# Attention and two expert layers in one kernel: the first batch's values loaded by ScalarE's queue, its keys by SyncE's

## The chip, the cores and the metric

The kernel runs on 1 core of one Trainium2 chip. The metric is the device time of one execution in microseconds (us). Three runs of the kernel before gave 496.34, 498.15 and 498.86 us, so the median is 498.15 us.

## The reference

Three parts follow each other. `q`, `k` and `v` have 4 batches, 8 heads, 576 positions and 64 values per head, all float32. Linear attention with a norm comes first, then a layer with a skip test and 8 experts (hidden size 1024), then a second layer with 8 experts and a capacity per expert. Only the first part is near the change:

```python
def _attn_ref(q, k, v, g_norm) -> np.ndarray:
    kv = np.einsum('bhsd,bhse->bhde', k, v)
    out = np.einsum('bhsd,bhde->bhse', q, kv)
    rms = np.sqrt(np.mean(out * out, axis=-1, keepdims=True) + 1e-06)
    return (out / rms * g_norm).astype(np.float32)
...
x = np.ascontiguousarray(attn_out.transpose(0, 2, 1, 3)).reshape(B * S, H * D)
x = _moe_ref(x=x, **moe_kwargs)
return _moe2_ref(x=x, **moe2_kwargs)
```

## The kernel before, in words

All keys of one batch are a table of 576 rows by 512 columns (8 heads side by side), and so are all values. A row of either is 2048 bytes. `load_kv(b)` brings one batch into SBUF: rows 0 to 511 of the keys go into the tile `wraw` (called `k0` in the code) as four chunks of 128 rows, the last 64 rows into the tile `k` (`k1`), and the values go the same way into another `wraw` (`v0`) and into `v` (`v1`). For the first batch each chunk is a DMA of its own of 256 KB, keys and values by turns; for the later batches a DMA holds two chunks. `load_q(b)` then brings the batch's queries, already transposed, as one DMA of 128 rows of 9216 bytes. All these DMAs are issued by SyncE (SP), in the order of the code: first batch, its queries, second batch, and so on. The order in which a queue issues is the order of the program; nothing here is placed by a planner.

ScalarE (ACT) issues two small DMAs at the start, `au` (gate weights and norm, 128 rows of 532 bytes, L116) and `cap_i` (the capacity, 8 bytes that are read once for each of 128 partitions, L118). Its first arithmetic of the attention is the copy at L701.

TensorE's order is written out by hand. It begins with ten matmuls on zeros (`warm`, L111), then does `emit_kv(0, range(5))` (L698): for chunks 0 to 3 and the last 64 rows, values against keys, summed in one PSUM tile. So each chunk needs its keys and its values. After the fifth chunk ACT copies the sums out (L701, L702), `emit_kvT` (L710, L713) transposes them and multiplies them with the gate weights, ACT copies these results (L715, L716), and `emit_products` (L732) multiplies queries with them, a tile of 128 rows at a time. The chunks of batch 1 are placed between the tiles of batch 0. VectorE (DVE), ACT and GpSimd (POOL) norm each tile, and SP stores it. The routing of the first expert layer starts while batch 3 is still in work, and the two expert layers fill the rest of the time.

Of the kernel before, what the change touches and what calls it, by code (L numbers as in the profile page):

```python
# [47 lines left out]
def moe_kernel(ctx: ExitStack, tc: tile.TileContext, qT, kk, vv, aux, w1a, w2a, w1b, w2b, capacity, out):  # L48
    nc = tc.nc
# [47 lines left out]
    for m, caps in ((1, CAP1), (2, CAP2)):  # L97
        t = cst.tile([1, E], F32, name=f"capc{m}")
# [538 lines left out]
    with att:  # L637
        warm(p1u.tile([128, 512], F32, name="acc"), 10)
        kvbd_all, vk_all = [], []
        for i in range(2):  # L640
            kvbd_all.append(asp0.tile([128, 4, 162], F32, name=f"kvbd{i}"))
            t = asp0.tile([128, 4, 128], F32, name=f"vk{i}")
# [5 lines left out]
        def load_kv(b):  # L648
            k0 = wr_p.tile([128, 2048], F32, name="wraw").rearrange("p (c d) -> p c d", c=4)
            v0 = wr_p.tile([128, 2048], F32, name="wraw").rearrange("p (c d) -> p c d", c=4)  # L650
            k1 = akv.tile([64, D], F32, name="k1")
            v1 = akv.tile([64, D], F32, name="v1")
            step = 1 if b == 0 else 2
            for c in range(0, 4, step):
                for t, src in ((k0, kk), (v0, vv)):
                    nc.sync.dma_start(out=t[:, c:c + step, :], in_=src[b, 0:512].rearrange("(c p) d -> p c d", c=4)[:, c:c + step, :])
            nc.sync.dma_start(out=k1, in_=kk[b, 512:576])
            nc.sync.dma_start(out=v1, in_=vv[b, 512:576])
            kt[b], vt[b] = (k0, k1), (v0, v1)

        def load_q(b):
# [7 lines left out]
        for b in range(B):  # L669
            load_kv(b)  # L670
            load_q(b)
# [97 lines left out]
        with tc.manual_schedule(engines={mybir.EngineType.PE}):  # L769
# [38 lines left out]
            for b in range(B):  # L808
                t = list(range((b * S) // 128 if b else 0, ((b + 1) * S) // 128))
                for u in ATT_SEQ[b].split():  # L810
# [13 lines left out]
                    elif u == "E":  # L824
                        p = tc.cur_priority
# [44 lines left out]
    with first_mix:  # L870
# [11 lines left out]
        for i in range(2):  # L882
            t = cst.tile([128, NB1, E], BF16, name=f"o2_{i}")
# [277 lines left out]
        step = tc.manual_schedule(engines={mybir.EngineType.PE})  # L1161
# [265 lines left out]
```

## Time and profile before

| | |
|---|---|
| runs before, us | 496.34, 498.15, 498.86 (median 498.15) |
| profiled execution, its own time | 496.94 us |
| its span, first to last instruction | 495.3 us |
| TensorE busy in the span | 472.5 us (95%) |
| mean granted TensorE clock | 0.982 of full |
| VectorE, ScalarE, GpSimd busy | 303.4, 205.8, 146.0 us |
| moved by DMA | 104.90 MB, 212 GB/s on average |

The table holds averages over the whole program. The change touches its first microseconds only, so the views to read are those of single stretches: who is busy, at what clock, what the DMA queues moved, and what the chain of work waited for. Queue q1 in the rows is the one that SP issues on, q10 the one that ACT issues on.

### The profile page before, as it was taken

Reading aid. Unit: us, or ns where it says so; the run is one execution under the profiler, and the core shown is the slowest. Engines: PE = TensorE matmul, PEld = TensorE weight load, DVE = VectorE, ACT = ScalarE, POOL = GpSimd, SP = SyncE. Lnnn points to the kernel's source line nnn. Section 1 sums busy time; section 2 is a strip of 40 time slices with the busy share of each in tenths; the row PEclk is TensorE's granted clock in tenths of the full one; section 3 lists DMA queues with packets and bytes.
Section 4 is the critical chain, followed back from the end, with each engine's and each line's share of the span. In section 5 each row is a group of like instructions: output and inputs, shape, how many; then the busy total and the mean of one; then the engine's idle time right before and its main releaser. Section 6 shows DMA issues by size and latency. Waiting matters only on the chain.

```text
span 495.3 us, 10239 instructions
## 1 busy us (share of the span) xinstructions
PE 472.5 (95%) x3824; PEld 450.7 (91%) x3829; DVE 303.4 (61%) x945; ACT 205.8 (42%) x524; POOL 146.0 (29%) x179
## 2 busy tenths in 40 slices
PE   6998778999999999999999999999999999999995
PEld 3897667999999999999998899999999999999984
DVE  2157978658767675265776576565657566675711
ACT  1376551344433532114233364454545545555400
POOL 5288584203021131113025230240604124040201
PEclk8599999999999999999999999999999999999999
DMA  8999495999768676358218993564656556400001
GB/s 236 362 356 347 163 355 154 315 323 348 269 229 299 206 290 210 126 194 314 91 45 304 414 336 142 193 202 150 214 187 221 201 179 215 144 37 2 35 23 41
DMA packets 24617, 104.90 MB, mean 212 GB/s; under 512 B 3609, under 2 KB 4761, under 8 KB 15984
## 3 DMA queue, kind: packets, MB, share of 16 engines
q1 hardware_dynamic: 17264, 77.75, 45.6%
q0 software_dynamic: 7008, 26.35, 15.1%
q8 instruction: 32, 0.52, 0.4%
q14 instruction: 25, 0.20, 0.1%
q10 hardware_dynamic: 288, 0.07, 0.1%
HBM read 92.15 MB, written 12.76 MB: 212 GB/s over the span
## 4 chain that ended last, share of the span: by engine, by line
PE 83%; DVE 8%; DMA 3%; ACT 2%; issue 2%; POOL 1%; SPq 0%; POOLq 0%; DVEq 0%; ACTq 0%
PE hp L592 14%; PE yp L1089 8%; PE yp L1091 8%; PE yp L1090 7%; PE hp L1089 6%; PE hp L1090 6%; PE hp L1091 6%; PE yp L626 6%; PE yp L616 6%; PE yp L617 2%; PE tp L1276 2%; PE yt L1320 2%; PE ops L732 2%; PE tp L1011 1%; PE tp L574 1%
## 5 line engine op out<-in xcount | busy, mean ns | idle before, releaser
L979 ACT CAST whi<-wraw 128x512 fp32r<-128x512 f32 x152 | 86.1, 619 | 73.3 <-PE yp L1090 30.1
L980 DVE TENSOR_TENSOR wlo<-wraw,whi 128x512 fp32r<-128x512 f32 x152 | 97.4, 684 | 26.1 <-ACT whi L979 25.0
L339 POOL DMA_INDIRECT rows<-xcat,gi x40 | 41.7, 1042 | 135.8 <-ACT ex L348 85.3
L1089 PE MATMUL hp<-xh,whi 128*128 128x256 f32 (+7 forms) x256 | 78.8, 308 | 0.2 <-DVE hl L1109 0.2
L592 PE MATMUL hp<-xT,wraw 128*128 128x128 f32 (+8 forms) x576 | 78.1, 292 | 0.5 <-ACT xT L576 0.5
L1091 PE MATMUL hp<-xh,wlo 128*128 128x256 f32 (+7 forms) x256 | 76.7, 299 | 0.0
L1090 PE MATMUL hp<-xl,whi 128*128 128x256 f32 (+7 forms) x256 | 76.6, 299 | 0.0
L592 PEld LDWEIGHTS hp<-xT,wraw 128*128 128x128 f32 x576 | 73.4, 190 | 2.9 <-issue 1.8
L1310 POOL DMA_INDIRECT out<-ot,toki x24 | 35.2, 1466 | 83.5 <-DVE su L352 39.5
L1089 PE MATMUL yp<-hh,whi 128*128 128x320 f32 (+5 forms) x192 | 58.8, 306 | 0.0
L1090 PE MATMUL yp<-hl,whi 128*128 128x320 f32 (+5 forms) x192 | 57.3, 298 | 0.0
L1091 PE MATMUL yp<-hh,wlo 128*128 128x320 f32 (+5 forms) x192 | 57.2, 298 | 0.0
L1089 PEld LDWEIGHTS hp<-xh,whi 128*128 128x128 f32 x256 | 48.3, 189 | 0.8 <-DVE hl L1109 0.5
L1090 PEld LDWEIGHTS hp<-xl,whi 128*128 128x128 f32 x256 | 48.3, 189 | 0.0
L1091 PEld LDWEIGHTS hp<-xh,wlo 128*128 128x128 f32 x256 | 48.3, 189 | 0.0
L1027 POOL DMA_INDIRECT xcat<-rows,toki x16 | 16.4, 1026 | 95.5 <-DVE mxt L297 93.1
L616 PE MATMUL yp<-hT,whi 128*128 128x352 f32 (+4 forms) x160 | 43.1, 351 | 0.0
L1108 ACT ACTIVATE hh<-hp 128x320 fp32r<-128x320 f32 (+8 forms) x64 | 27.2, 429 | 31.7 <-PE hp L1091 24.1
L1109 DVE SCALAR_TENSOR_TENSOR hl<-hp,hh 128x320 fp32r<-128x320 f32 (+8 forms) x64 | 30.0, 475 | 13.4 <-ACT hh L1108 12.8
L617 PE MATMUL yp<-hT,wlo 128*128 128x176 f32 (+4 forms) x160 | 37.7, 235 | 0.0
L1090 PEld LDWEIGHTS yp<-hl,whi 128*128 128x128 f32 x192 | 36.2, 189 | 0.0
L1089 PEld LDWEIGHTS yp<-hh,whi 128*128 128x128 f32 x192 | 36.2, 188 | 0.0
(255 smaller groups left out, 867.2 us busy)
## 6 DMA issues: line engine op xcount, KB each, us to landing
wraw<-in_w1a SPq DMA_DIRECT2D x14, 1024.0 KB
wraw<-in_w2a SPq DMA_DIRECT2D x14, 1024.0 KB, 5.6
wraw<-in_w1b SPq DMA_DIRECT2D x14, 1024.0 KB
wraw<-in_w2b SPq DMA_DIRECT2D x14, 1024.0 KB, 5.2
xcat<-xr SPq DMA_DIRECT2D x18, 264.0 KB, 3.9
q<-in_q SPq DMA_DIRECT2D x3, 1152.0 KB
wraw<-in_k SPq DMA_DIRECT2D x6, 512.0 KB, 10.2
wraw<-in_v SPq DMA_DIRECT2D x6, 512.0 KB, 12.8
```

Of the source, the lines that this page charges most:

```text
L339: return nc.gpsimd.indirect_dma_start(out=rows[:n], out_offset=None, in_=xcat[0:source], in_offset=bass.IndirectOffsetOnAxis(ap=gi[:n], ax ...
L592: nc.tensor.matmul(hp[:, ff, :], lhsT=wv[:, fc % 4, k, :], rhs=XT[j][:, k, c0:c1], start=(k == 0), stop=(k == 3))
L616: nc.tensor.matmul(yp, lhsT=wh[:, fc, :], rhs=HT[j][:, fc], start=(fc == 0), stop=False, skip_group_check=True)
L617: nc.tensor.matmul(yp[:, 0, :], lhsT=wl[:, fc, :], rhs=HT[j][:, fc, 0, :], start=False, stop=(fc == 7), skip_group_check=True)
L626: nc.tensor.matmul(yp[:, dd, :], lhsT=wv[:, dd, fc, :], rhs=HT[j][:, fc, c0:c1], start=(fc == 0), stop=(fc == 7))
L979: nc.scalar.copy(out=hi[:, cs], in_=raw[:, cs])
L980: ins = nc.vector.tensor_tensor(out=lo[:, cs], in0=raw[:, cs], in1=hi[:, cs].bitcast(F32), op=ALU.subtract)
L1089: nc.tensor.matmul(ps, lhsT=wh, rhs=xh, start=first, stop=False)
L1090: nc.tensor.matmul(ps, lhsT=wh, rhs=xl, start=False, stop=False)
L1091: nc.tensor.matmul(ps, lhsT=wl, rhs=xh, start=False, stop=last)
L1109: ev = nc.vector.scalar_tensor_tensor(out=hl[:, fs, cs], in0=hp, scalar=0.0, in1=hh[:, fs, cs].bitcast(F32), op0=ALU.max, op1=ALU.subtract)
L1310: st = nc.gpsimd.indirect_dma_start(out=out, out_offset=bass.IndirectOffsetOnAxis(ap=r2["toki"][:nn, j, bi:bi + 1], axis=0), in_=ot[:nn], ...
```

## The change

In `load_kv`, for the first batch alone, the four chunks of the values and their last 64 rows are issued by ACT instead of SP. The keys of the first batch, the queries and all later batches stay with SP. An empty line is added, so line numbers below it are one higher in the changed kernel.

```diff
             step = 1 if b == 0 else 2
             for c in range(0, 4, step):
                 for t, src in ((k0, kk), (v0, vv)):
-                    nc.sync.dma_start(out=t[:, c:c + step, :], in_=src[b, 0:512].rearrange("(c p) d -> p c d", c=4)[:, c:c + step, :])
+
+                    (nc.scalar if b == 0 and t is v0 else nc.sync).dma_start(out=t[:, c:c + step, :], in_=src[b, 0:512].rearrange("(c p) d -> p c d", c=4)[:, c:c + step, :])
             nc.sync.dma_start(out=k1, in_=kk[b, 512:576])
-            nc.sync.dma_start(out=v1, in_=vv[b, 512:576])
+            (nc.scalar if b == 0 else nc.sync).dma_start(out=v1, in_=vv[b, 512:576])
```

SP's first instructions in the kernel before, at the start of the program (`k_209`, `v_210` are the last 64 rows of batch 0, `q_221` its queries, 128x2x512 a double chunk of batch 1):

```order
L656 DMA wraw<-in_k 128x512
L656 DMA wraw<-in_v 128x512
...
L657 DMA k_209<-in_k 64x512
L658 DMA v_210<-in_v 64x512
L664 DMA q_221<-in_q 128x2304
L656 DMA wraw<-in_k 128x2x512
```

The same place on SP in the changed kernel:

```order
L657 DMA wraw<-in_k 128x512 x4
L658 DMA k_209<-in_k 64x512
L665 DMA q_221<-in_q 128x2304
L657 DMA wraw<-in_k 128x2x512
L657 DMA wraw<-in_v 128x2x512
```

The five DMAs of the values are gone from SP, and the queries are its 6th DMA instead of its 11th.

ACT's first instructions in the changed kernel (the two copies of `vk_197` are its first arithmetic of the attention):

```order
L116 DMA au<-in_aux 128x133
L114 ACT_TABLE_LOAD
L114 ACTIVATE act_127<-eps_123 128x1
L118 DMA cap_i<-in_capacity 128x2
L657 DMA wraw<-in_v 128x512 x4
L659 DMA v_210<-in_v 64x512
L702 COPY vk_197<-acc 64x4x64
L703 COPY vk_197<-acc 64x4x64
```

The five DMAs stand behind `au` and `cap_i` and ahead of the first copy; the order of all other instructions, on every engine, is as before.

## Rows read from the trace of the kernel before

**Rows 1.** The page: span, and granted TensorE clock in 40 slices.
```profile
span 495.3 us, 10239 instructions
...
PEclk8599999999999999999999999999999999999999
```

**Rows 2.** Chain that ended last, 0 to 32 us: start us, us, what.
```profile
1.79 5.35 DMA wraw<-in_k
...
7.16 5.16 DMA v<-in_v
...
17.52 2.53 PE ops L732 x8
...
26.75 1.30 PE ops L732 x8
```

**Rows 3.** Timeline, 0 to 14 us: start us, us, engine, line; in brackets idle before, releaser.
```profile
0.87 0.41 ACTq L116 DMA_DIRECT2D au<-in_aux  x1
...
1.37 0.40 ACTq L118 DMA_DIRECT2D cap_i<-in_capacity  x1
...
3.21 0.43 SPq L656 DMA_DIRECT2D wraw<-in_v  x1
...
6.07 0.77 PE L698 MATMUL acc<-wraw 128*64 128x64 f32 x16
...
7.16 0.48 SPq L658 DMA_DIRECT2D v<-in_v  x1
...
7.68 0.58 SPq L664 DMA_DIRECT2D q<-in_q  x1
...
11.09 1.12 PE L698 MATMUL acc<-wraw 128*64 128x64 f32 x16 [0.94 <-DMA wraw<-in_v]
...
12.46 1.12 PE L698 MATMUL acc<-k,v 64*64 64x64 f32 x16 [0.25 <-DMA v<-in_v]
...
13.68 0.37 ACT L701 COPY vk<-acc 64x256 f32<-64x256 f32 x1 [10.87 <-PE acc L698]
```

**Rows 4.** DMA queues, 0 to 6 us: packets, MB, share of 16 engines.
```profile
q1 hardware_dynamic: 340, 0.63, 47.7%
q10 hardware_dynamic: 288, 0.07, 6.9%
```

**Rows 5.** DMA queues, 4 to 6 us.
```profile
q1 hardware_dynamic: 102, 0.18, 64.3%
q10 hardware_dynamic: 105, 0.00, 2.5%
```

**Rows 6.** DMA queues, 2.3 to 3.4 us.
```profile
q1 hardware_dynamic: 131, 0.24, 62.8%
q10 hardware_dynamic: 134, 0.06, 29.9%
```

**Rows 7.** DMA packets, 6 to 10 us.
```profile
DMA packets 880, 1.59 MB, mean 398 GB/s; under 512 B 102, under 2 KB 102, under 8 KB 880
```

**Rows 8.** DMA packets, 10 to 11.5 us.
```profile
DMA packets 117, 0.37 MB, mean 245 GB/s; under 512 B 25, under 2 KB 25, under 8 KB 92
```

**Rows 9.** DMA queues, 12 to 13.5 us.
```profile
q1 hardware_dynamic: 66, 0.61, 97.3%
```

**Rows 10.** Stretches: us, PE, PEld, DVE, ACT, POOL busy (x), PEclk, DMA share, GB/s.
```profile
5.92:13.58 7.66, 4.53 (x81) 3.91 (x82) 2.38 (x15) 0.00 (x0) 5.26 (x22) 0.75 1.05 356
13.58:17.52 3.94, 3.25 (x13) 2.59 (x14) 0.00 (x0) 1.59 (x4) 0.00 (x0) 0.50 1.01 384
17.52:23.35 5.83, 5.83 (x45) 5.38 (x46) 1.57 (x4) 1.58 (x4) 2.03 (x2) 0.50 1.07 344
31.00:43.00 12.00, 11.95 (x171) 11.14 (x170) 6.90 (x18) 8.86 (x25) 10.52 (x10) 1.00 1.02 331
43.00:61.00 18.00, 12.89 (x129) 11.18 (x131) 17.54 (x63) 9.65 (x28) 11.19 (x11) 1.00 0.67 235
...
78.00:495.00 417.00, 408.88 (x3201) 396.73 (x3200) 256.34 (x786) 169.61 (x430) 96.50 (x87) 1.00 0.56 195
```

## The prediction, made before the changed kernel ran

> **What bounds the kernel now.** I read the page first, then the chain that ended last, the timeline of the first 14 us, the DMA queues in short windows, and the table of stretches.
>
> The page says that the program is one long stretch of TensorE work at full clock, with a dip of the granted clock in its second slice [rows 1]. The table of stretches shows where a delay at the start could be lost: from 78 us to the end TensorE is busy 408.88 of 417 us, from 31 to 43 us 11.95 of 12, and between them, from 43 to 61 us, VectorE 17.54 of 18 [rows 10]. There is little idle time on whichever engine sets the pace, so I expect a microsecond lost before 30 us to arrive at the end nearly whole.
>
> The chain of the first 17 us is made of loads: it runs through a key chunk, issued at 1.79 us, and then through the last 64 rows of the values, issued at 7.16 us and waited for until 12.32 us [rows 2]. The first chunk's matmuls start at 6.07 us, the fourth chunk's wait 0.94 us for the values, and the fifth's 0.25 us more [rows 3]. What follows (sums copied out, transposes, first products at 17.52 us) is a chain in which nothing waits for a DMA.
>
> Two things about the DMAs matter. From 6 to 10 us they are full: 1.59 MB at 398 GB/s [rows 7]. Before 6 us they are not: SP's queue has moved 0.63 MB and ACT's 0.07 MB [rows 4]. In the last 2 us of that, the two queues moved 102 and 105 packets, with only 0.18 MB in all [rows 5]; the packets of ACT's queue are here the 8-byte reads of `cap_i`. In 2.3 to 3.4 us, with 2048-byte packets on SP's queue and 532-byte ones on ACT's, it was 131 and 134 [rows 6]. So while both queues have work, they advance packet for packet, whatever the packets' sizes. That is what the forecast rests on.
>
> **The change part by part.** (1) Five issues leave SP. With them gone the queries are SP's 6th DMA. The 6th was issued at 3.21 us without a stall, while the 10th and 11th (last values, queries) came at 7.16 and 7.68 us [rows 3]. So the queries are in SP's queue by about 3.7 us, before the DMAs are full. As issue time SP's saving is worth nothing: from 6 us on the DMAs have no idle time that earlier issues could fill [rows 7].
>
> (2) Five issues are added to ACT, each about 0.43 us as on SP, 2.2 us together, from 1.77 us (the end of the `cap_i` issue) to about 4 us. ACT's first copy waits 10.87 us for TensorE and starts at 13.68 us [rows 3], so they are hidden. Without that cover they would cost at most the 2.2 us.
>
> (3) The order in which the bytes arrive changes, and this is the term. Keys and values of the batch are 576 rows of 2048 bytes each, 1.18 MB each; the queries are 1.18 MB in 128 packets of 9216 bytes, 8 for each of the 16 DMA engines. Before, one queue delivered everything in the order of need. By 6.00 us 0.63 MB of 2.36 MB was there [rows 4]; the other 1.73 MB take 4.35 us at 398 GB/s [rows 7], to 10.35 us. The window with the 64-row transfers and the first query packets ran at 245 GB/s instead of 398 [rows 8], which loses 1.5 x (398 - 245) / 398 = 0.58 us, so to 10.9 us. The wait ended at 12.32 us [rows 2]: the slowest engine was 1.4 us behind that mean.
>
> After, the values stand behind `au` and `cap_i` in ACT's queue, and these 288 packets are through only at 6 us [rows 4]. SP's queue will have moved the same 0.63 MB by then, but all of it keys. From 6.00 us:
> - The other 0.55 MB of keys go packet for packet with 0.55 MB of values: 1.10 MB, 2.76 us, to 8.76 us. Then 0.63 MB of values are left, 308 packets.
> - SP's next work is the queries. Their 128 packets go with 128 value packets: 1.18 + 0.26 = 1.44 MB, 3.62 us, to 12.4 us. That a query packet does cost what its size says is seen where they run alone: 66 packets took 97.3% of 16 engines for 1.5 us, 0.35 us each [rows 9].
> - The 180 value packets left go with 180 of batch 1's keys: 0.74 MB, 1.85 us, to 14.2 us; with the same 0.58 us for the 64-row transfers, 14.8 us.
>
> If no engine is behind that mean, the last values are 14.8 - 12.32 = 2.5 us later; if the slowest is again 1.4 us behind, 3.9 us. The engines fell behind before 6 us, when the values have not begun, and the exchange packet for packet lets an engine that is behind with its keys go on with its values. I take 2.6 us, near the lower end. From below, nothing excludes a gain: if the values kept their place and the tail went away, they would be there 1.4 us sooner (10.9 instead of 12.32). The ends of this term are so -1.4 and +3.9 us.
>
> (4) From there the work is the same, 2.6 us later: the fifth chunk at about 15.1 us and the first products at about 20.1 us instead of 17.52. The granted clock is at 0.50 (1.2 GHz) in the stretches 13.58 to 17.52 us and 17.52 to 23.35 us, and TensorE had idle time in the first and none in the second before the clock rose [rows 10]. The same products take 2.53 us at that level and 1.30 us at the full one [rows 2]. If the clock rises later by as much as the uninterrupted work starts later, the whole 2.6 us are carried on. If it rises at 23.35 us as now, 2.6 us of work at the half level are replaced by work at the full one, and 1.3 us remain.
>
> (5) The loads of the later batches keep their order, and SP reaches them earlier. They bring the same bytes; batch 1's keys come beside the end of the values, and their matmuls are moved back too. I cost this at nothing.
>
> The sum is +2.6 us. The profiled execution took 496.94 us, with a span of 495.3 us, which is 1.2 us below the median of 498.15 us. It would become 499.5 us; for a median of runs I add the same to 498.15 us and forecast 500.8 us.
>
> **The rivals.**
> - **Half of it:** the delay is there, but the clock rises at the old moment, so 1.3 us remain: 499.5 us. For it: the profile shows two levels with a late rise, not a rise tied to an instruction. Against it: the rise came only after a stretch without any idle time, and the small wait for ACT before the products would then lie later.
> - **No change:** the place of the values in the transfers isn't moved, since the engines have the same bytes to bring; 498.15 us. Against it: the equal packet counts. The Trainium skill, "DMA: Bandwidth & Descriptors", section "Issuing engines are not separate DMA queues", has this rule: DMAs started by different engines run on the same 16 engines and interleave, and starting them from several saves only the issue time. By that rule nothing would be gained, and that the full window has no room for issue time agrees [rows 7]; the rule doesn't say what the interleaving does to the one transfer that is waited for.
> - **Faster:** SP's last value issue at 7.16 us was late because SP's queue was held up, and with two queues the last values are out by 4 us. If the exchange leaves them ahead of the queries, they land at 10.9 us and 1.4 us are gained: 496.75 us. If TensorE then also has fewer pauses between 5.92 and 13.58 us (it is busy 4.53 of 7.66 us there) and its clock stays up, the 9.08 us of busy time in the two stretches at 0.50 shrink by up to 4.5 us: 492.2 us [rows 10]. The point from which it decides is whether the values are through before the queries. For it: each chunk's keys and values travel side by side. Against it: in SP's queue only 36 packets of keys per engine stand ahead of the queries, so packet for packet they are reached before the values' 36 are done.
> - **Slower still:** the tail of 1.4 us stays too, 3.9 us are lost and carried whole: 502.05 us.
>
> **How the numbers follow.** The forecast has 0.38, half of it 0.20, no change 0.17, faster 0.14, slower still 0.11. A measurement of this kernel can tell about 0.5%, 2.5 us, from no change, so the border lies at 500.6 us. The forecast is a hair above it: I give 0.28 of its 0.38 to the slower side, with the 0.11 of the last rival 0.39. Half, no change and the small form of the faster case (0.05) make, with the forecast's other 0.10, 0.52. The large form of the faster case is 0.09. The range reaches from 497.4 us (the faster case's small gain in part, and the scatter of the runs) to 502.6 us (the last rival, and some scatter); it leaves out the large gain and the far end above.
>
> **What would show it.** Right: queue q10 in the changed profile holds some 1.2 MB, moved mostly between 6 and 15 us; in that time q1 moves the queries; the fourth and fifth chunks' matmuls wait for values by over 2 us more, the first chunk starts after 7 us, and the first products come at about 20 us. The chain then runs through a value DMA issued by ACT. Wrong: the last values landing before 12.3 us, or equal landing with the time changed. A delay at 20 us that is gone at 78 us would show step (4) wrong, and a wait of the first copy on ACT for anything but TensorE would show step (2) wrong.

## The result, and the profile after

The changed kernel took 501.11 us (median of 5 runs, 500.58 to 501.79). The kernel before took 497.51 us (5 runs, 496.34 to 498.86). The ratio is 1.007, with a 95% interval of 1.0043 to 1.0098: slower by 3.6 us. A second measurement, `e11_changed_again` below, gave 1.009 (1.0064 to 1.0116).

The page of the changed kernel, first the span, then the two queues (packets, MB, share of 16 engines):

```profile
span 498.9 us, 10244 instructions
...
q1 hardware_dynamic: 16608, 76.57, 44.7%
...
q10 hardware_dynamic: 944, 1.25, 0.7%
```

The span is 3.6 us longer than in [rows 1], and ACT's queue q10 now carries 1.25 MB: the change does what it says. The first 23 us of the changed kernel's timeline answer to [rows 3] (start us, us, engine; "q" behind an engine marks its DMA issues):

```profile
0.88 1.82 SPq L657 DMA_DIRECT2D wraw<-in_k  x4
...
1.81 0.45 ACTq L657 DMA_DIRECT2D wraw<-in_v  x1
...
3.94 0.33 SPq L665 DMA_DIRECT2D q<-in_q  x1
...
4.12 0.33 ACTq L657 DMA_DIRECT2D wraw<-in_v  x1
...
6.12 0.33 ACTq L657 DMA_DIRECT2D wraw<-in_v  x1
...
8.30 0.33 ACTq L657 DMA_DIRECT2D wraw<-in_v  x1
...
8.67 0.53 ACTq L659 DMA_DIRECT2D v<-in_v  x1
...
8.78 1.13 PE L699 MATMUL acc<-wraw 128*64 128x64 f32 x16 [2.85 <-DMA wraw<-in_v]
...
13.28 1.12 PE L699 MATMUL acc<-wraw 128*64 128x64 f32 x16 [3.38 <-DMA wraw<-in_v]
...
16.27 1.12 PE L699 MATMUL acc<-wraw 128*64 128x64 f32 x16 [0.59 <-DMA wraw<-in_v]
...
17.32 1.12 PE L699 MATMUL acc<-k,v 64*64 64x64 f32 x16
...
18.55 0.37 ACT L702 COPY vk<-acc 64x256 f32<-64x256 f32 x1 [15.72 <-PE acc L699]
...
22.39 2.53 PE L733 MATMUL ops<-kvbd,q 128*128 128x162 f32 x8 [0.36 <-ACT kvbd L717]
```

Two things are to be seen. TensorE waits for values at four of the five chunks; the fifth chunk begins at 17.32 instead of 12.46 us, the first products at 22.39 instead of 17.52 us, 4.87 us later. And ACT does not issue its value DMAs one behind the other: after the first at 1.81 us they come at 4.12, 6.12, 8.30 and 8.67 us, while the queries leave SP at 3.94 us.

The trace also has what spaces the issues. The loads of this program signal their landing on eight semaphores (counters that a landing DMA raises and an instruction can wait for), which SP and ACT share and use in turn. In every run, the first eight loads of the two engines together go out without a wait, and in the 14 us looked at each further one goes only when the load that had its semaphore before has landed. In the kernel before, the eight were six of SP and two of ACT; in the changed kernel they are five of SP and three of ACT. SP's waits, in the kernel before (0 to 8 us):

```profile
SPq L656 <- DMA au<-in_aux: 0.4, 1, 0.4
```

and in the changed kernel (0 to 14 us):

```profile
SPq L657 <- DMA wraw<-in_v: 2.6, 1, 2.6
...
SPq L665 <- DMA wraw<-in_k: 0.6, 1, 0.6
```

The first and the second are issues of SP that wait for a load of ACT; the third is the queries, which wait for the first key chunk. ACT's issues at 4.12, 6.12 and 8.30 us follow in the same way the landings of the gate weights and of SP's second and third key chunk, which were issued at 0.88, 1.33 and 1.80 us and took 3.2, 4.8 and 6.5 us to land.

The DMA queues of the changed kernel show what that does. From 0 to 6 us (against [rows 4]):

```profile
q1 hardware_dynamic: 337, 0.62, 46.6%
q10 hardware_dynamic: 294, 0.08, 6.5%
```

From 7.6 to 8.5 us:

```profile
q1 hardware_dynamic: 124, 0.34, 128.5%
q10 hardware_dynamic: 11, 0.01, 3.3%
```

From 9 to 11 us:

```profile
q1 hardware_dynamic: 73, 0.66, 82.7%
q10 hardware_dynamic: 71, 0.15, 19.3%
```

Until 6 us SP's queue moved 0.62 MB, all keys, and ACT's hardly more than its two small loads. From 7.6 to 8.5 us hardly any values moved (11 packets of ACT's queue, 0.01 MB, the end of the first chunk), although the second value chunk had been issued at 4.12 us; the queries, issued 0.18 us before it, were starting. (A share above 100% is possible because a packet is counted whole in the window in which it starts.) From 9 to 11 us the queues moved 73 and 71 packets, but 0.66 MB of one and 0.15 MB of the other: each 2048-byte packet of values took its turn with a 9216-byte packet of queries.

The delay goes on into the rest. The clock column of this execution cannot be used before 28 us (it says 1.00, while the products took the 2.53 us that they took at half clock before [rows 2]); the repeat has it. Its stretches, in the columns of [rows 10]:

```profile
13.58:17.52 3.94, 3.34 (x54) 2.86 (x52) 0.00 (x0) 0.00 (x0) 0.00 (x0) 0.50 1.05 351
17.52:23.35 5.83, 5.47 (x33) 4.35 (x31) 0.00 (x0) 1.59 (x4) 0.00 (x0) 0.50 1.06 364
23.35:31.00 7.65, 7.65 (x108) 6.93 (x107) 3.92 (x11) 4.71 (x12) 4.52 (x4) 0.87 1.06 359
```

The clock is still at 0.50 (1.2 GHz) at 23.35 us, where it rose before, and 0.87 in the next stretch: about 2 us more at the half level.

### The profile page after: what moved, and what is told of

Same layout as the page of the kernel before. It is cut to its first block, busy times and chain, and to the rows that moved or that the text cites. A ratio compares the mean times of both kernels' runs of the same rounds, so it can differ in the third digit from the quotient of the medians.

```text
span 498.9 us, 10244 instructions
## 1 busy us (share of the span) xinstructions
PE 475.8 (95%) x3829; PEld 452.7 (91%) x3829; DVE 303.2 (61%) x945; ACT 205.6 (41%) x524; POOL 143.4 (29%) x179
## 3 DMA queue, kind: packets, MB, share of 16 engines
q10 hardware_dynamic: 944, 1.25, 0.7%
## 4 chain that ended last, share of the span: by engine, by line
PE 77%; DVE 2%; DMA 1%; ACT 0%; issue 0%; POOL 0%; POOLq 0%; ACTq 0%
PE hp L592 14%; PE yp L1090 7%; PE yp L1092 7%; PE yp L1091 7%; PE hp L1090 7%; PE hp L1091 6%; PE hp L1092 6%; PE yp L616 6%; PE yp L626 5%; PE yp L617 2%; PE tp L1277 2%; PE yt L1321 2%; PE tp L1012 1%; PE tp L574 1%; DMA rows<-xcat,gi 1%; PE lg L999 1%
## 5 line engine op out<-in xcount | busy, mean ns | idle before, releaser
L1311 POOL DMA_INDIRECT out<-ot,toki x24 | 32.8, 1368 | 83.8 <-DVE su L352 39.9
## 6 DMA issues: line engine op xcount, KB each, us to landing
wraw<-in_v SPq DMA_DIRECT2D x6, 512.0 KB, 11.5
```

What stands on the lines that cost most here:

```text
L1311: st = nc.gpsimd.indirect_dma_start(out=out, out_offset=bass.IndirectOffsetOnAxis(ap=r2["toki"][:nn, j, bi:bi + 1], axis=0), in_=ot[:nn], ...
```

## The experiments

Three theories. **A:** the two queues advance packet for packet, so the large query packets on SP's queue hold the values back. **B:** it is ACT's issue; its queue lets value DMAs out late, and where the queries are does not matter. (That the late issues are waits for one of the eight semaphores was not known to the theories.) **C**, formed after the first eight runs: both together; ACT's late issue puts value DMAs behind the queries, what SP issued earlier is served first, and then it goes packet for packet. All ratios are to the kernel before on the same chip, with 5 rounds; 95% intervals in brackets. None of these kernels leaves out work.

**e1_q_act: the queries behind the values, on ACT.**

```diff
             if b < B - 1:
-                nc.sync.dma_start(out=q0, in_=qT[b])
+                (nc.scalar if b == 0 else nc.sync).dma_start(out=q0, in_=qT[b])
```

> The changed kernel, but the first batch's queries are issued by ScalarE too, behind the values. Theory A (the two queues advance packet for packet, and SyncE's 9216-byte query packets push the values back): nothing big stands beside the values any more, only batch 1's keys of the same packet size, so the fifth chunk's matmuls start at 12.5 to 14 us instead of 17.3, and the time is 497.5 to 499 us. Theory B (ScalarE's queue issues the values late, at 4.1, 6.1 and 8.3 us, whatever SyncE's queue holds): the start stays at 16 us or later and the time at 500 to 501 us.

Measured: 1.0024 [1.0011, 1.0037], the fifth chunk at 15.39 us. That is 1.9 us sooner than in the changed kernel and later than A allowed. The value DMAs were again issued late (1.80, then from 4.51 to 8.78 us), and batch 1's first keys, which moved up to 4.30 us on SP, took the queries' place ahead of them. The time of 499.64 us lies between A's and B's too. Neither A nor B alone.

**e2_q_parts: the queries in smaller packets.**

```diff
+            if b == 0:
+                for hp in range(4):
+                    nc.sync.dma_start(out=q0[:, hp, :], in_=qT[b][:, hp, :])
-            if b < B - 1:
+            elif b < B - 1:
                 nc.sync.dma_start(out=q0, in_=qT[b])
```

> The changed kernel, but the first batch's queries are four DMAs with packets of 2304 instead of 9216 bytes, at the same place in SyncE's queue. The bytes are the same, only the packets are smaller. Theory A: the values get about half of the transfer while the queries run, instead of a fifth; the fifth chunk starts at 12.7 to 14.5 us and the time is 497.7 to 499.3 us. A rival in which the queues share by bytes, and theory B: no difference from the changed kernel, 17 us and 501 us.

Measured: 1.0026 [1.0003, 1.0049]. The fifth chunk's and the products' lines of the timeline:

```profile
14.23 0.68 PE L702 MATMUL acc<-k,v 64*64 64x64 f32 x16 [0.92 <-DMA v<-in_v]
...
17.66 1.37 PE L736 MATMUL ops<-kvbd,q 128*128 128x162 f32 x8 [0.36 <-ACT kvbd L720]
```

The same bytes in the same place of the same queue, in packets of a quarter, bring the fifth chunk from 17.32 to 14.23 us. That is inside A's range, and against B alone. But the run does not tell packet size from place: the four DMAs leave SP at 3.93, 7.52, 7.89 and 9.18 us, so only the first quarter of the queries stood ahead of the second to fourth value chunks (4.11, 6.07 and 6.44 us). Against sharing by bytes speak the equal packet counts above, not this run. The products ran here at full clock (1.37 us); the time over the runs lay between 495.66 and 502.35 us, wider than for most others, and the profiled execution is the fastest of them.

**e3_small_sp: the two small loads on SP, ahead of the keys.**

```diff
-    nc.scalar.dma_start(out=au, in_=aux)
+    nc.sync.dma_start(out=au, in_=aux)
...
-    nc.scalar.dma_start(out=cap_i, in_=capacity.bitcast(I32).unsqueeze(0).to_broadcast([128, 2]))
+    nc.sync.dma_start(out=cap_i, in_=capacity.bitcast(I32).unsqueeze(0).to_broadcast([128, 2]))
```

> The changed kernel, but the gate weights and the capacity are issued by SyncE, ahead of the keys, so that ScalarE's queue holds the values alone. Theory A: now the keys lag and the queries stand behind them, so nothing that is needed later overtakes the values or the keys; the fifth chunk starts at 11 to 13 us, the time is 496 to 498 us. Theory B: the last values are still issued after about 8 us, the start is 14 us or later and the time 498.5 us or more.

Measured: 1.0008 [0.9986, 1.003]; the fifth chunk at 13.19 us. In the compiled order the last 64 rows also came first on ACT. The lines that matter:

```profile
3.02 0.33 ACTq L657 DMA_DIRECT2D wraw<-in_v  x1
...
7.22 0.34 ACTq L657 DMA_DIRECT2D wraw<-in_v  x1
...
8.37 0.33 SPq L665 DMA_DIRECT2D q<-in_q  x1
...
13.19 1.12 PE L699 MATMUL acc<-k,v 64*64 64x64 f32 x16
```

Values still on ACT's queue, its last DMA still issued late (7.22 us), but ahead of the queries (8.37 us): 4 us of the delay are gone. B's 14 us fell; A's 13 us was missed by a little. The time, 498.79 us where the kernel before took 498.54 on that chip, decides nothing between them.

**e5_after_cap_late: the capacity out of the way.**

```diff
-    nc.scalar.dma_start(out=cap_i, in_=capacity.bitcast(I32).unsqueeze(0).to_broadcast([128, 2]))
...
-    nc.vector.tensor_copy(out=capf, in_=cap_i[:, 0:1])
...
             load_q(b)
+        nc.sync.dma_start(out=cap_i, in_=capacity.bitcast(I32).unsqueeze(0).to_broadcast([128, 2]))
...
             att.close()
+            nc.vector.tensor_copy(out=capf, in_=cap_i[:, 0:1])
```

> The changed kernel, but the capacity is loaded behind all loads of the attention, at about 40 us, so that only the gate weights stand ahead of the values. If the slow 8-byte reads at 3.4 to 6 us are what leaves the values behind: both queues run at about 400 GB/s from 2.6 us, the values lag by less than a us, the fifth chunk starts at 9.5 to 11.5 us and the time is 495 to 497 us. Theory B: the values are still issued one by one as earlier transfers of ScalarE's queue land, the start is 13 us or later and the time 498 us or more.

Measured: 1.0064 [1.0041, 1.0088]; the fifth chunk at 14.70 us. My expectation was wrong; the numbers are those expected of B (13 us or later, 498 us or more). The start of the loads is much better (the second chunk at 7.16 us), and then this happens:

```profile
3.79 0.33 SPq L663 DMA_DIRECT2D q<-in_q  x1
...
3.98 0.33 ACTq L655 DMA_DIRECT2D wraw<-in_v  x1
...
5.06 0.33 ACTq L655 DMA_DIRECT2D wraw<-in_v  x1
...
6.81 0.53 ACTq L657 DMA_DIRECT2D v<-in_v  x1
...
12.12 1.12 PE L698 MATMUL acc<-wraw 128*64 128x64 f32 x16 [4.27 <-DMA wraw<-in_v]
```

The third chunk waits 4.27 us for values that were issued at 3.98 us, 0.19 us behind the queries. The queues of this run from 8.5 to 10.5 us:

```profile
q1 hardware_dynamic: 76, 0.70, 84.4%
q10 hardware_dynamic: 74, 0.15, 19.7%
```

The same exchange as in the changed kernel, 76 packets against 74. So the slow start is not what the change costs; that it is the place of the values behind the queries was argued here, and e9 and e10 tested it.

**e6_q_held: the queries held to 7.55 us.**

```diff
             q0 = aq.tile([128, 4, S], F32, name="q0")
+            if b == 0:
+                with tc.high_priority():
+                    nc.vector.tensor_copy(out=q0[:, 0, 0:1], in_=capf)
```

with all later loads of SP kept behind the queries, as in e9 and e10.

> The changed kernel, with both queues and their order as they are, but SyncE's query DMA has to wait for a tiny VectorE copy that itself waits for the capacity (about 6.3 us), and all later loads stay behind it. Theory A in the form that the runs so far suggest (a transfer also starts only after those issued before it on the other queue, and then the queues go packet for packet; the queries were issued at 3.9 us, ahead of the second value chunk): all five value DMAs are now issued before the queries, the fifth chunk's matmuls start at 11 to 13.5 us instead of 17.3, the time is 496 to 499 us. Theory B (ScalarE's queue itself lets a value DMA out only as an earlier one of its own lands): the values are issued at 4.1, 6.1 and 8.3 us as before, the fifth chunk starts at 14 us or later, the time is 499.5 us or more.

Measured: 1.0066 [1.0041, 1.0092], the fifth chunk at 17.00 us: B's numbers, not A's. But the timeline shows why:

```profile
7.55 0.33 SPq L676 DMA_DIRECT2D q<-in_q  x1
...
8.22 0.33 ACTq L659 DMA_DIRECT2D wraw<-in_v  x1
...
15.95 1.12 PE L714 MATMUL acc<-wraw 128*64 128x64 f32 x16 [2.94 <-DMA wraw<-in_v]
```

The hold was too short. Three value chunks came out ahead of the queries, and the second and third began together at 11.03 us; the fourth was issued 0.67 us behind the queries and was waited for until 15.95 us. Hence theory C, and the runs e9 and e10.

**e4_cap_late: the kernel before with the capacity late** (the edit of e5 on the kernel before).

> The kernel before (values and keys on SyncE's queue by turns), but with the capacity loaded behind all loads of the attention, at about 40 us. If its 8-byte reads are what empties the DMAs at 3.6 to 5.6 us, the loads run at about 400 GB/s from 2.6 us on, the fifth chunk starts at 9.5 to 11 us instead of 12.5, and the time falls by 1 to 3 us. If something else does (the first touch of each table, say), the start stays at 12 us or later and the time is that of the kernel before.

Measured: 0.9979 [0.996, 0.9997], the fifth chunk at 10.75 us, faster than the kernel before. The DMA packets of this run from 4 to 6 us, where the kernel before moved 0.18 MB [rows 5]:

```profile
DMA packets 425, 0.78 MB, mean 388 GB/s; under 512 B 46, under 2 KB 46, under 8 KB 425
```

So the load of the capacity, 128 reads of 8 bytes of one address, had held the other loads back there; how it does so was not tried.

**e7_two_queues: two queues, nothing ahead of the values.** The edit of e5, and the gate weights behind the values:

```diff
-    nc.scalar.dma_start(out=au, in_=aux)
+    au_load = nc.scalar.dma_start(out=au, in_=aux)
...
+            if b == 0:
+                behind(ins, last)
+                behind(au_load, ins)
```

> Values on ScalarE's queue, keys on SyncE's, but the gate weights stand behind the values and the capacity is loaded at about 40 us, so nothing is ahead of the values and they are issued before the queries. Theory A: the two queues bring keys and values side by side in the order of need, like the one queue of the run with the late capacity: the fifth chunk starts at 9.5 to 11.5 us, the time is 494.5 to 497.5 us, within 1 us of that run. Theory B, or a second queue that costs something by itself: the start is 13 us or later, the time 498.5 us or more.

Measured: 1.0005 [0.9985, 1.0024], the fifth chunk at 13.28 us, later than expected. ACT issued its fourth chunk at 4.44 us and the last 64 rows at 5.55 us; the queries went at 4.63 us between them. The fourth chunk was waited for until 11.74 us. Missed, and for C's reason as far as the last rows go. The fourth chunk was issued ahead of the queries, so C does not cover it; why it came so late was not tried.

**e8_last_rows_only: the last 64 rows alone on ACT.**

```diff
-            nc.sync.dma_start(out=v1, in_=vv[b, 512:576])
+            (nc.scalar if b == 0 else nc.sync).dma_start(out=v1, in_=vv[b, 512:576])
```

> One part of the change alone, on the kernel before: only the last 64 rows of the first batch's values are issued by ScalarE, the four chunks stay with SyncE. Theory A: this small DMA is issued at 1.8 us, long before the queries, and lands by about 8 us; the fourth chunk, still on SyncE's queue, sets the end, the fifth follows it at 12 to 12.5 us, and the time is that of the kernel before within 0.2%. If the mere use of a second queue costs, the fifth chunk starts 1 us or more later than 12.5 us and the time rises by 1 us or more.

Measured: 1.002 [1.0003, 1.0037], the fifth chunk at 13.30 us. The fourth chunk came at 12.25 instead of 11.09 us. So A's "same" was a little too good: the small DMA costs about 1 us at the start. The fourth chunk's values on SP were issued at 5.71 us in place of 4.45, with no order changed. ACT's third load is one of the first eight, so SP has five of them instead of six, and this issue now waits until the first value chunk has landed (issued at 1.32 us, 4.4 us to landing).

**e9_cap_late_q_held: e5 with the queries held** until VectorE's constants are done.

```diff
+            if b == 0:
+                nc.vector.tensor_copy(out=q0[:, 0, 0:1], in_=sum4[:, 0:1])
```

> The run with the late capacity and the values on ScalarE's queue (fifth chunk at 14.7 us), with one thing changed: SyncE's query DMA waits for a VectorE copy at the end of the constants, about 7 us, so that all value DMAs (issued by 6.8 us in that run) are issued ahead of it; all later loads stay behind the queries. Theory C (what SyncE issues before a value DMA is served before it, and then packet for packet; ScalarE's queue takes only some three of these DMAs at a time, so its later values are issued late): no value stands behind the queries any more, the fifth chunk starts at 10 to 12 us and the time is 495 to 498 us. If the second queue costs by itself, or its issue is all that counts: 14 us or later, as without the hold, and a time 2 us or more above the kernel before.

Measured: 0.9975 [0.9959, 0.9992].

```profile
4.00 0.82 ACTq L657 DMA_DIRECT2D wraw<-in_v  x2
...
5.03 0.53 ACTq L663 DMA_DIRECT2D v<-in_v  x1
...
7.65 0.33 SPq L673 DMA_DIRECT2D q<-in_q  x1
...
8.68 0.69 PE L712 MATMUL acc<-wraw 128*64 128x64 f32 x16 [1.26 <-DMA wraw<-in_v]
...
10.16 0.68 PE L712 MATMUL acc<-k,v 64*64 64x64 f32 x16
...
13.60 1.37 PE L746 MATMUL ops<-kvbd,q 128*128 128x162 f32 x8 [0.36 <-ACT kvbd L730]
```

All value DMAs are out at 5.03 us, the queries at 7.65 us, and the fifth chunk starts at 10.16 instead of 14.70 us. The edit adds to e5 only the hold, which keeps SP's later loads behind the queries too. By it the last values are also issued sooner (5.03 instead of 6.81 us), because the queries no longer take one of the eight semaphores ahead of them. The third chunk tells the two effects apart: its values were issued at 3.98 us in e5 and at 4.00 us here, and its matmuls start at 12.12 and at 8.68 us.

**e10_q_held_longer: the changed kernel with the same hold.** The edit of e9 on the changed kernel.

> The changed kernel with its query DMA held until the end of VectorE's constants, about 8.8 us, when the last value DMA (8.7 us in the changed kernel) has just been issued; the hold to 7.55 us had left the last two value DMAs behind the queries, and the fifth chunk at 17.0 us. Theory C: the fifth chunk starts at 12 to 14 us instead of 17.3, and the time is 1 us or less above the kernel before. If the queries' place does not matter, 16 us or later and 3 us or more above it.

Measured: 1.0008 [0.9984, 1.0032].

```profile
4.22 0.33 ACTq L659 DMA_DIRECT2D wraw<-in_v  x1
...
7.53 0.53 ACTq L665 DMA_DIRECT2D v<-in_v  x1
...
8.80 0.33 SPq L675 DMA_DIRECT2D q<-in_q  x1
...
9.77 2.83 PE L713 MATMUL acc<-wraw 128*64 128x64 f32 x48 [0.69 <-DMA wraw<-in_v]
...
12.53 0.74 PE L713 MATMUL acc<-k,v 64*64 64x64 f32 x16
```

With the queries 1.3 us behind the last values, the fifth chunk is back at 12.53 us (12.46 in the kernel before), and the time is not to be told from that of the kernel before. Both queues and the slow start are still there, and so is most of ACT's late issue (7.53 instead of 8.67 us at the end). The second chunk's values were issued at 4.22 us, even later than the 4.12 us of the changed kernel, and its matmuls start at 9.77 instead of 13.28 us. This settles it: the change costs what it costs because value DMAs stand behind loads that SP issued ahead of them, the queries here, and at a smaller price batch 1's keys in e1.

**e11_changed_again: the changed kernel, same chip as e9 and e10.**

> The changed kernel itself once more, beside the two runs with held queries on the same chip: every theory expects what it gave before, the fifth chunk at 16.5 to 18 us and a time 2.5 to 4.5 us above the kernel before.

Measured: 1.009 [1.0064, 1.0116], the fifth chunk at 17.15 us, as before.

All runs together, by the fifth chunk's start (the starts are of one profiled execution each):

| kernel | fifth chunk, us | first products, us | ratio |
|---|---|---|---|
| e9: late capacity, queries held | 10.16 | 13.60 | 0.9975 |
| e4: one queue, late capacity | 10.75 | 15.38 | 0.9979 |
| before | 12.46 | 17.52 | 1 |
| e10: changed, queries held to 8.8 | 12.53 | 16.02 | 1.0008 |
| e3: small loads on SP | 13.19 | 18.26 | 1.0008 |
| e7: small loads out of the way | 13.28 | 18.35 | 1.0005 |
| e8: last rows only | 13.30 | 18.37 | 1.002 |
| e2: queries in parts | 14.23 | 17.66 | 1.0026 |
| e5: changed, late capacity | 14.70 | 19.77 | 1.0064 |
| e1: queries on ACT | 15.39 | 20.46 | 1.0024 |
| e6: queries held to 7.55 | 17.00 | 22.07 | 1.0066 |
| changed, second time | 17.15 | 22.22 | 1.009 |
| changed | 17.32 | 22.39 | 1.007 |

The times do not follow the starts closely. e5 gains 2.6 us at the fifth chunk and is hardly faster than the changed kernel, and e1, which starts later than e5, is faster. Single executions drift by a microsecond or more behind the start: TensorE's first matmul of the routing (L178, L176 in e5) comes at 76.32 us in e1 and at 77.40 us in e5. What makes this difference was not taken apart.

## Why the prediction was right, step by step

The direction was right, and so was the exchange packet for packet as the main term; the time (501.11 us, 500.8 forecast) lies in the range. The change itself was 3.6 us where 2.6 was forecast; the chance of over 0.5% slower was put at 0.39, below the 0.52 for no clear change, and it is what came. That the total is so close is partly luck: the forecast added its 2.6 us to 498.15 us, where the kernel before took 497.51 us in five runs, and the small gap hides larger ones in the terms.

- **Step (1), SP.** Right in the number, not in its reason: the queries left SP at 3.94 us (3.7 forecast), but not without a stall. They waited 0.6 us for the first key chunk to land. SP's shorter list saved nothing.
- **Step (2), ACT.** Half right. The five issues are hidden from ACT's own work: its first copy still waits for TensorE alone, now 15.72 us. But I had them out by about 4 us, and they came at 1.81, 4.12, 6.12, 8.30 and 8.67 us. The row that I took the spacing from was SP's, whose six went in a row because they and ACT's two were the first eight. That a later issue waits for a landing stood in [rows 2]: the key chunk issued at 1.79 us took 5.35 us, until 7.14 us, and the last values were issued at 7.16 us. This is the step that failed, and it is what puts four of the five value DMAs behind the queries in the order of issue; e9 and e10 show what that is worth.
- **Step (3), the exchange.** Right in kind: 0.62 MB of keys by 6 us (0.63 forecast), then packet for packet (73 against 71). The size was too small: the fifth chunk is 4.86 us later, above the upper end of 3.9 that I had set for the delay and well above the 2.6 that I took. About 0.9 us of the excess is the stretch from 7.6 to 8.5 us in which hardly any values moved; by theory C it comes from step (2). The rest, about 1.4 us, is a tail: by the sum the values would all be there at 14.8 us, and the last rows, issued at 8.67 us, took 8.4 us to land, until 17.1 us. A tail of 1.4 us is what the prediction had found in the kernel before and left out. I had reasoned that the engines that lag would catch up; they did not, and no run here took that apart. The waits also fell elsewhere than was named as a sign: the fourth chunk waited 0.59 us and the fifth not at all, but the first 2.85 and the second 3.38 us.
- **Step (4), the clock and the carrying.** The clock rose later, as forecast: in the repeat it is at 0.50 until after 23.35 us. The 4.87 us at the first products became 3.6 us at the end. In both executions TensorE's first matmul of the routing behind the attention (L178) can be found, at 74.91 us before and at 79.52 us after, so 4.6 us are still there and about 1 us goes later, in the expert layers. The repeat of the changed kernel has 78.31 us there, 3.4 us later than before, and a span that is 6.3 us longer (501.6 us). So the delay is carried to 80 us in the main; what it loses or gains from there, single executions do not tell.
- **Step (5), the later loads.** Right: the waits of TensorE in the first 18 us are for batch 0's values only, and no matmul of batch 1's chunks shows a wait for a load.

Of the rivals, "no change" and "faster" fell with the first view of the queues, and "half of it" with the clock. "Slower still" (3.9 us, 502.05 us) is the closest to the delay that was found, but not for its reason alone. The rule of the Trainium skill that was quoted ("DMA: Bandwidth & Descriptors", "Issuing engines are not separate DMA queues") holds in what it says: the best run with two queues (e9, 0.9975) and the one with one queue (e4, 0.9979) cannot be told apart. What it leaves out decided here: which transfer is served when.

Two versions beat both kernels: e4 and e9, each about 1 us faster than the kernel before, with intervals that only just exclude no change. In e4 it comes from moving the capacity's load alone; e9 has the second queue as well and gains no more by it.

## What to carry to other kernels

Splitting one stream of loads over two queues gives up its order: here the queues then took turns by packets, and a large transfer that nobody needed yet got ahead of a small one that was waited for. Before moving a DMA, write down when each queue really issues and which landing each issue waits for (the timeline and the waits of the DMA queue have it; an issue on one engine can wait for a load of the other), and hold back on the other queue whatever is not urgent until the urgent ones are out. Look also for tiny reads at the start: they may cost more than the loads that you rearrange.

## What was not expected of the hardware

- A second queue let no more loads out. In every run eight loads of SP and ACT together went out without a wait (six and two in the kernel before, five and three in the changed one, seven and one in e4), and then one for each landing. So ACT's value chunks waited for SP's keys; it was not, as theory C had put it, ACT's queue that takes three at a time. The eight are semaphores of this program; their number was not varied.
- A DMA issued 0.18 us behind the queries on the other queue moved nothing for 4.4 us. Until 7.8 us the chunk ahead of it in its own queue was moving; from there to 8.5 us ACT's queue had 2 packets (0.00 MB), while the queries started. In e5, where it was 0.19 us, ACT's queue moved no packet at all from 6.5 to 7.9 us.
- 128 reads of 8 bytes from one address held the loads down to 0.18 MB in 2 us, where 0.78 MB moved without them (e4).
- In e9, with shorter waits at the start, the first products ran at full clock (1.37 us at 13.60 us, 2.53 us before), without anything being done for it. By the end about 1.1 us (by the medians) of the 3.9 us that its profiled execution was ahead at that point were left.
